# Zero fills of two stages issued in pairs, and w_down moved in 2-KB rows

## The chip, the core and the metric

The kernel runs on one core of one Trainium2 chip. The metric is the device time of one execution in microseconds (us), as the median of several runs. TensorE (PE), VectorE (DVE), ScalarE (ACT) and GpSimd (POOL) compute; SyncE (SP) and POOL issue transfers. Sixteen DMA engines carry out all transfers of the core, whichever engine issued them.

## What is computed

The reference is one decode step of a transformer block and its gradients for all inputs but one:

```
mod = (silu(c) @ w_mod) -> sa, ca, ga, sb, cb, gb          # six vectors of 1024
h = layernorm(x) * (1 + ca) + sa
x = x + ga * (attention(h @ wq, K, V) @ wo)                # last W = 4096 of 65536 cache rows
h = layernorm(x) * (1 + cb) + sb
x = x + gb * ((sigmoid(h @ w_gate) * (h @ w_up)) @ w_down) # F = 3584
out = x, and the vjp with grad_out for x, K, V, wq, wo, w_gate, w_up, w_down, c, w_mod
```

There is one query row, 32 query heads, 4 key/value heads of width 128, and D = 1024. The gradients of the two caches have 4 x 65536 x 128 elements in bf16 each. Only the last 4096 rows of each head are not zero. So 120 MB (in units of 1024 x 1024 bytes) of the outputs are zeros that must still be written, and they are about half of all bytes that move.

## The kernel before

**Zero fills.** The regions that are zero are cut into 120 pieces of 1 MB: 8 head regions of 15 pieces. A piece is `[128 partitions x 4096 bf16]`, 8 KB per partition. The source is one small tile, `zeros`, of 2 KB per partition in an 8-bit type, which the DMA widens to 32 bits as it writes. The list `zleft` holds the pieces in order. Eight of them are "narrow": they are written as two transfers[...] (L160 to L165). The other 112 are "wide", one transfer each (L169). `zero(n, after)` takes n pieces off the list and issues them from POOL. If `after` is given, the first waits for that matmul, so that fills are paced by the progress of TensorE.

**The stages.** All engines execute fixed orders of instructions, written by hand. In the order of time the stages are:

- loads, modulation vectors, transposes of K and wq, scores and softmax (to about 75 us), with 8 fills (`Z_Q`, `Z_SM`);
- **N** (about 75 to 155 us): 128 steps s, each with two matmuls at L635; in every step `zero(Z_N[s], recent(mm, 6))` issues fills that wait for the matmul of five steps before;
- **B** (about 155 to 270 us): 48 chunks of eight matmuls at L687; each ends in `zero(Z_B[chunk], recent(mm, 3))`. Three fills stand in its middle (`Z_GA`);
- **CB and FOLD** (about 270 to 303 us): three fills (`Z_CB`), then `fold_tile` (L882), the loads of the first two feed-forward blocks (`load_ug`, L869) and the fills of `Z_FOLD`;
- **the feed-forward blocks** (about 295 to 480 us): seven blocks q of 512 columns. For each, `front` (L933) and `ffn_mm` (L950) are the forward products, `wd_ttr` and `wd_outer` make the gradient of w_down in place, and a loop over j makes those of w_up and w_gate in place. `store_wd` (L859) and `store_ug` (L873) write them out from POOL. `load_wd` (L856) is issued from SP and waits until the store of the block before has left the buffer. `dug_part` spreads a vector over the partitions, with a copy on ACT at L970. Each block has 4 fills, the last two blocks 6 (`Z_FFN`);
- **the end** (from about 480 us): gradients of wo, w_mod, K, V and wq, with the last fills (`Z_END`, and what is left in the list).

**Queues.** POOL issues 273 transfers into one queue. Each of these transfers counts on one of eight semaphores in turn, and a POOL transfer waits until the one eight before it has landed. SP has a queue of its own.

**w_down.** Row 2p and row 2p + 1 of a half block of 256 rows lie on partition p, so that a partition's piece of 4 KB is contiguous in memory. For the same reason `front` takes every second column of w_up and w_gate, and the copy at L970 permutes its elements.

Of the kernel before, what the change touches and what calls it, by code (L numbers as in the profile page):

```python
# [10 lines left out]
P = 128  # L11
FP32 = mybir.dt.float32
# [10 lines left out]
FB = 512  # L23
# [17 lines left out]
def spread(total, n):  # L41
    return [(i + 1) * total // n - i * total // n for i in range(n)]
# [7 lines left out]
Z_Q = [0] * 6 + [1, 3]  # L50
Z_KC = [0] * 8
Z_SM = 4
Z_N = spread(29, 128)
Z_B = spread(29, 43) + [1, 1, 1, 1, 0]
Z_FOLD = (3, 2, 2)
Z_FFN = [(1, 1, 1, 1)] * 5 + [(1, 1, 2, 2), (2, 2, 1, 1)]
Z_END = (2, 1, 1, 0, 0)
@with_exitstack
def kernel(
# [26 lines left out]
    nc = tc.nc  # L86
# [17 lines left out]
    def vt(shape, name, dt=FP32):  # L104
        return pool.tile(shape, dt, name=name)
# [4 lines left out]
    ZW = 4096  # L110
    zeros = vt([P, ZW // 2], "zeros", FP8)
# [11 lines left out]
    zregions = []  # L123
    for og in (out_2, out_3):
        for g in range(G):
            region = og[0, g, 0:SKW, :].rearrange("r d -> (r d)").rearrange("(p x) -> p x", p=P)
            for i in range(region.shape[1] // ZW):
                zregions.append(region[:, i * ZW:(i + 1) * ZW])

    narrow = zregions[0:len(NARROW)]
# [1 line left out]
    zleft = []  # L133
# [13 lines left out]
    def dep(later, earlier):  # L147
        tc.add_manual_dep(later.ins, earlier.ins.name,
                          mybir.DependencyInfo(mybir.DependencyClass.Sync, mybir.DependencyReason.DATA),
                          reason="pace")  # L150

    def zero(n, after=None):
        for _ in range(n):
            if len(zleft) <= keep[0]:
                return
            region, narrow_ = zleft.pop(0)
            first = None
            if narrow_:
                nc.gpsimd.inc_swdge_sem([], [], mode="reset_dge_cursor")  # L160
                n = nlen - ncount.pop()
                first = nc.gpsimd.dma_start(
                    out=rest[0:NS, 0:nlen * 128].rearrange("p (t x) -> p t x", t=2)[:, :, n * 64:(n + 1) * 64],
                    in_=zeros[0:NS, 0:64].rearrange("p (t x) -> p t x", t=1).broadcast_to([NS, 2, 64]))
                ins = nc.gpsimd.dma_start(  # L165
                    out=region[8:P, :].bitcast(FP32).rearrange("(t p) x -> p t x", t=2),
                    in_=zeros[0:60, :].rearrange("p (t x) -> p t x", t=1).broadcast_to([60, 2, ZW // 2]))
            else:
                ins = nc.gpsimd.dma_start(out=region.bitcast(FP32), in_=zeros[:, :])  # L169
            if after is not None:  # L170
                dep(first or ins, after)

# [15 lines left out]
    def new_tp(name="tp"):  # L188
        p, tag = next_pool()
        return p.tile([P, 1024], BF16, name=name, tag=tag)  # L190
# [214 lines left out]
    for j in range(KD):  # L405
        for k in range(16):
            mm = nc.tensor.matmul(mod_ps[:, k:k + 1], lhsT=wm01_t[j][:, k * P:(k + 1) * P],
                                  rhs=cs_bf[:, j:j + 1], start=(j == 0 and k == 0), stop=(j == KD - 1),
                                  skip_group_check=True)
# [53 lines left out]
    for j in range(KD):  # L463
# [6 lines left out]
        for h in range(HQ):  # L470
            mm = nc.tensor.matmul(q_ps[:, h:h + 1], lhsT=wq_t[j][:, h * P:(h + 1) * P],  # L471
                                  rhs=h1_bf[:, j:j + 1], start=(j == 0 and h == 0), stop=(j == KD - 1),
                                  skip_group_check=True)
# [9 lines left out]
    for ch in range(8):  # L483
        ps = new_ps("sc_ps")
        for g in range(G):
            mm = nc.tensor.matmul(ps[32 * g:32 * g + 32, 0:512], lhsT=q_col2[:, HG * g:HG * g + 32],
                                  rhs=k_T[:, g, ch * 512:(ch + 1) * 512], start=True, stop=True,
                                  tile_position=(0, 32 * g))
# [19 lines left out]
    for tb in range(4):  # L508
# [3 lines left out]
        tp = new_tp("tp_pT")  # L512
# [107 lines left out]
    def recent(mm, lag):  # L620
        last_mm.append(mm)
        return last_mm[-lag] if len(last_mm) >= lag else last_mm[0]

    for g in range(G):
        nbank = bank_pair("n_ps", g)
        for t_ in range(KT):
            s = g * KT + t_
            vp = vp_t[(s // 2) % 2]
            if t_ % 2 == 0:
                tt(vp.rearrange("p t h d -> p (t h d)"),  # L630
                   v_nat[:, g, t_ * DH:(t_ + 2) * DH].rearrange("p (t o d) -> p t o d", t=2, o=1).broadcast_to([P, 2, HG, DH]),
                   pT2[:, g, HG * t_:HG * t_ + 2 * HG, :].rearrange("p n (o k) -> p n o k", o=1).broadcast_to([P, 2 * HG, 64, 2]),
                   ALU.mult)
            for k in range(2):
                mm = nc.tensor.matmul(nbank[k][:, :], lhsT=k_nat[:, g, t_ * DH:(t_ + 1) * DH],  # L635
                                      rhs=vp[:, t_ % 2, 4 * k:4 * k + 4, :].rearrange("p h d -> p (h d)"),
                                      start=(t_ == 0), stop=False)
            zero(Z_N[s], recent(mm, 6))
            if t_ == 20:
                build_bd(g)  # L640
            if s == 2:
                ok_cols(ok4)
            elif s == 4:
                ok_rows()
            elif s == 24:
                mod_gb()
            elif t_ % 2 == 1:
                side()
        for k in range(2):
            nc.tensor.matmul(nbank[k][:, :], lhsT=nkb_rows[:, :], rhs=bd[:, 4 * k:4 * k + 4, :].rearrange("p h d -> p (h d)"),  # L650
                             start=False, stop=True)
            c0 = (HG * g + 4 * k) * P
            nc.scalar.activation(out=N_sb[:, c0:c0 + 512], in_=nbank[k][:, :], func=ACT.Copy, scale=float(SCALE))
        load_wo(4 + g, nc.gpsimd if g == 3 else nc.sync)
        if g < 3:
            jobs.extend(t_unit(h, "AA") for h in range(HG * g, HG * g + HG))
# [5 lines left out]
    bq = []  # L662
# [11 lines left out]
    nbq = len(bq)  # L674
    bbank = {}

    def bch(n=1):
        for _ in range(n):
            if not bq:
                return  # L680
            p, i, u = bq.pop(0)
            if i == 0:
                bbank[p] = bank_pair("b_ps", p)
            for a in range(4):
                h = 4 * u + a
                for k in range(2):
                    mm = nc.tensor.matmul(bbank[p][k][:, :], lhsT=a4[:, p, h, :], rhs=wo_t[u][:, a, k * 512:(k + 1) * 512],  # L687
                                          start=(i == 0 and a == 0), stop=(i == 7 and a == 3))
            zero(Z_B[nbq - 1 - len(bq)], recent(mm, 3))
            if i == 7:  # L690
                for k in range(2):
                    o = B_t[p][:, k * 512:(k + 1) * 512]
                    if k == 0 or p == NBP - 1:
                        nc.scalar.copy(out=o, in_=bbank[p][k][:, :])
                    else:
                        cp(o, bbank[p][k][:, :])
# [152 lines left out]
    ug_v = arena[:, 16 * KIB:48 * KIB].rearrange("p (h q j k f) -> p q h j k f", h=2, q=2, j=4, k=2)  # L849
    wd_v = ar(152, 8).rearrange("p (i d) -> p i d", i=4)  # L850

    def wd_dram(t, q, s):
        return t[q * FB + s * 256:q * FB + s * 256 + 256, :].rearrange("(p j) d -> p j d", j=2)

    def load_wd(q, s):
        nc.sync.dma_start(out=wd_v[:, 2 * s:2 * s + 2, :], in_=wd_dram(B_w_down, q, s))  # L856
# [40 lines left out]
    load_ug(0, 4, 4)  # L897
    zero(Z_FOLD[0])
    side(2)
# [12 lines left out]
    load_ug(1, 4, 4)  # L912
    zero(Z_FOLD[1])
    bcast(dffn_bf, KD, b1k, "AV")

    dug_b = scr
# [10 lines left out]
    def front(q):  # L927
        gu = gu_t[q % 2]
        for col, k in ((4, 0), (0, 1)):
            for i in range(4):  # L930
                f0 = 256 * (i // 2) + i % 2
                for j in range(KD):
                    nc.tensor.matmul(gu[:, col + i:col + i + 1], lhsT=ug_v[:, q % 2, j // 4, j % 4, k, f0:f0 + 255:2],  # L933
                                     rhs=h2_bf[:, j:j + 1], start=(j == 0), stop=(j == KD - 1))

    def gates(q):
# [26 lines left out]
    def dug_part(q):  # L963
        r = small[q % 2]
        mulv(r["dug_bf"][:, 0:4], r["dhh"], r["sg"])
        mulv(r["dug_bf"][:, 4:8], r["dhh"], r["hom"])
        tp = new_tp("tp_dug")
        for i in range(8):
            nc.tensor.transpose(tp[:, i * P:(i + 1) * P], r["dug_bf"][:, i:i + 1].broadcast_to([P, P]), ident_bf[:, :])
        nc.scalar.copy(out=dug_b.rearrange("p (s f j) -> p s f j", s=4, j=2),  # L970
                       in_=tp.rearrange("p (s j f) -> p s f j", s=4, j=2))

    for h in range(HQ):
        jobs.append(tr_unit(wo_t[h // 4][:, h % 4, :]))
# [9 lines left out]
    ffn_mm(0, 1)  # L984
    wd_ttr(0, 1)
    dug_part(0)
    wd_outer(0, 1)
    zero(Z_FOLD[2])
    load_wd(1, 0)
    load_wd(1, 1)  # L990
    for q in range(NB):
# [290 lines left out]
    s2(6)  # L1282
    s2(7)
    keep[0] = 0
    zero(len(zleft))
    assert not zleft and not narrow and not jobs and not bq

# [28 lines left out]
```

## Time and profile before

| | |
|---|---|
| median of three runs | 603.95 us (603.56 to 604.6) |
| the profiled execution | 604.6 us, of which 602.8 us are the span shown |
| bytes moved by DMA | 248.19 MB in 47730 packets |
| HBM read, written | 61.87 MB, 185.60 MB |
| zero fills | 112 of 1024 KB and 8 of 960 KB, median 13.9 and 13.1 us from issue to landing |
| w_down loads | 14 of 512 KB, median 9.7 us from issue to landing |
| busy: PE, DVE, ACT, POOL | 65%, 54%, 47%, 29% |

The page divides the span into 40 slices of 15.07 us. In its row "DMA", 9 means that the 16 DMA engines were busy for at least 90% of the slice; the row "GB/s" is what they moved in it. A landing is the moment at which the last of the 16 DMA engines has reported. In a timeline, the square brackets hold the idle time of the engine just before the instruction, and what ended it.

### The profile page before, as it was taken

The page shows a single profiled execution, that of the slowest core. Times are in us where ns is not written, and L with a number is a line of the kernel's source. Part 1 is how long each engine was busy: PE and PEld are TensorE (multiplying, and loading weights), DVE is VectorE, ACT ScalarE, POOL GpSimd, SP SyncE. Part 2 cuts the span into 40 slices and gives each one's busy share as a digit, 9 for nine tenths or more (in the row PEclk, how much of TensorE's full clock was granted, in tenths as well). Part 3 has the DMA queues.
Part 4 walks back from the last instruction along what each step waited for, and adds up shares of the span by engine and source line. Part 5 has one row for each costly group of instructions (what it writes and reads, how often), then busy time and mean ns, then how long its engine had stood idle before and what let it go on. Part 6 is the DMA issues. An engine that isn't in the chain of part 4 may idle for free.

```text
span 602.8 us, 10936 instructions
## 1 busy us (share of the span) xinstructions
PE 389.8 (65%) x4516; PEld 265.6 (44%) x4516; DVE 324.8 (54%) x616; ACT 282.8 (47%) x426; POOL 174.2 (29%) x281
## 2 busy tenths in 40 slices
PE   3997789999999989989433434352533377837200
PEld 3995434334344445548433433342433255736200
DVE  3654498999511010060374675846768279678510
ACT  2489514567202014218273847657476834744100
POOL 0002121212322212213334454455443431132230
PEclk9999699999999989989755555555555586655555
DMA  8999999999999999999999999999999999999996
GB/s 351 421 417 421 406 426 413 413 417 422 421 422 427 423 426 419 407 426 417 406 413 411 412 415 413 413 409 410 414 416 421 422 419 411 423 424 426 424 415 256
DMA packets 47730, 248.19 MB, mean 412 GB/s; under 512 B 5629, under 2 KB 5629, under 8 KB 27264
## 3 DMA queue, kind: packets, MB, share of 16 engines
q0 software_dynamic: 37792, 210.78, 91.0%
q1 hardware_dynamic: 9840, 36.71, 18.0%
q8 instruction: 35, 0.57, 0.4%
q14 instruction: 15, 0.12, 0.1%
q10 hardware_dynamic: 48, 0.01, 0.0%
HBM read 61.87 MB, written 185.60 MB: 411 GB/s over the span
## 4 chain that ended last, share of the span: by engine, by line
DMA 35%; PE 34%; DVE 14%; issue 7%; ACT 5%; POOL 2%; ACTq 0%; POOLq 0%; DVEq 0%; SPq 0%
DMA out_dram<-arena 17%; PE b_ps L687 14%; DMA out_dram<-zeros 8%; DMA arena<-in_B_w_down_dram 7%; PE n_ps L635 6%; DVE arena L210 4%; DVE arena L193 4%; PE t_ps L597 2%; DMA arena<-in_B_w_up_dram 2%; DVE arena L206 2%; DVE junk L210 2%; ACT arena L241 2%; PE tp_wq L453 2%; PE w_ps L394 1%; PE tp_k L434 1%
## 5 line engine op out<-in xcount | busy, mean ns | idle before, releaser
L169 POOL DMA_DIRECT2D out_dram<-zeros x112 | 61.1, 546 | 205.6 <-PE q_ps L471 50.2
L687 PE MATMUL b_ps<-arena 128*128 128x512 bf16 x384 | 89.5, 389 | 0.0
L836 PE MATMUL tp_side<-ident_bf,arena 128*128 128x128 bf16 x416 | 50.1, 297 | 53.7 <-ACT arena L837 44.6
L193 DVE TENSOR_TENSOR arena<-arena 128x2048 bf16<-128x2048 bf16 x64 | 76.6, 1224 | 2.2 <-PE n_ps L635 0.3
L837 ACT COPY arena<-tp_side 128x1024 bf16<-128x1024 bf16 x52 | 52.0, 1010 | 46.0 <-PE tp_side L836 45.8
L210 DVE CUSTOM_DVE_ANT_0 arena<-arena,scr 128x1024 bf16<-128x1024 bf16 x56 | 65.2, 1221 | 9.5 <-ACT scr L970 9.5
L635 PE MATMUL n_ps<-arena 128*128 128x512 bf16 x256 | 65.7, 378 | 6.5 <-DVE arena L193 4.8
L836 PEld LDWEIGHTS <-arena 128*128 128x128 bf16 x416 | 41.2, 137 | 59.2 <-issue 59.1
L241 ACT ACTIVATE arena<-scr,h 128x1024 bf16<-128x1024 bf16 x56 | 61.0, 1146 | 0.0
L687 PEld LDWEIGHTS <-arena 128*128 128x128 bf16 x384 | 37.7, 100 | 46.4 <-issue 7.1
L873 POOL DMA_DIRECT2D out_dram<-arena x42 | 30.7, 733 | 43.9 <-ACT arena L241 36.7
L635 PEld LDWEIGHTS <-arena 128*128 128x128 bf16 x256 | 24.6, 97 | 41.8 <-issue 16.4
L210 DVE CUSTOM_DVE_ANT_0 junk<-arena,b1k 128x1024 bf16<-128x1024 bf16 x28 | 34.3, 1223 | 15.9 <-DMA arena<-in_B_w_down_dram 15.4
L1137 ACT ACTIVATE arena<-ps_kv 128x512 bf16<-128x512 f32 x48 | 26.2, 694 | 29.8 <-PE ps_kv L1133 26.0
L599 ACT CAST arena<-t_ps 128x512 bf16<-128x512 f32 x56 | 30.1, 589 | 12.1 <-PE t_ps L597 12.1
L1133 PE MATMUL ps_kv<-junk,arena 8*128 8x128 bf16 x256 | 27.5, 306 | 10.1 <-DVE arena L206 9.4
L1133 PEld LDWEIGHTS <-arena 8*128 8x128 bf16 x256 | 25.5, 141 | 11.9 <-issue 11.9
L202 DVE CAST arena<-b_ps 128x512 bf16<-128x512 f32 x5 | 3.5, 692 | 47.1 <-PE b_ps L687 47.1
L933 PE MATMUL fg<-h_bf,arena 128*128 128x1 bf16 x448 | 15.6, 166 | 19.0 <-DMA arena<-in_B_w_up_dram 12.4
L455 ACT COPY arena<-tp_wq 128x1024 bf16<-128x1024 bf16 x23 | 21.7, 1044 | 8.0 <-PE tp_wq L453 8.0
L950 PE MATMUL fg<-hh_bf,arena 128*128 128x1 bf16 x224 | 8.0, 166 | 24.1 <-DMA arena<-in_B_w_down_dram 23.4
L933 PEld LDWEIGHTS <-arena 128*128 128x128 bf16 x448 | 14.4, 105 | 20.2 <-DMA arena<-in_B_w_up_dram 13.0
(297 smaller groups left out, 640.0 us busy)
## 6 DMA issues: line engine op xcount, KB each, us to landing
out_dram<-zeros POOLq DMA_DIRECT2D x112, 1024.0 KB, 13.9
out_dram<-arena POOLq DMA_DIRECT2D x32, 1024.0 KB, 18.8
out_dram<-arena POOLq DMA_DIRECT2D x36, 512.0 KB, 10.3
arena<-in_A_wq_dram SPq DMA_DIRECT2D x8, 1024.0 KB, 20.0
out_dram<-zeros POOLq DMA_DIRECT2D x8, 960.0 KB, 13.1
arena<-in_B_w_down_dram SPq DMA_DIRECT2D x14, 512.0 KB, 9.7
out_dram<-arena POOLq DMA_DIRECT2D x28, 256.0 KB, 10.9
arena<-in_A_wo_dram SPq DMA_DIRECT2D x6, 1024.0 KB, 24.8
```

The lines of the kernel that those rows point to most:

```text
L169: ins = nc.gpsimd.dma_start(out=region.bitcast(FP32), in_=zeros[:, :])
L193: return nc.vector.tensor_tensor(out=out, in0=a, in1=b, op=op)
L210: return nc.vector.tensor_tensor_reduce(out=out, in0=w, in1=b, scale=1.0, scalar=0.0, op0=ALU.mult, op1=ALU.add, accum_out=acc)
L241: return nc.scalar.activation(out=out, in_=b, func=ACT.Copy, scale=col)
L599: nc.scalar.copy(out=o, in_=ps)
L635: mm = nc.tensor.matmul(nbank[k][:, :], lhsT=k_nat[:, g, t_ * DH:(t_ + 1) * DH], rhs=vp[:, t_ % 2, 4 * k:4 * k + 4, :].rearrange("p h d -> ...
L687: mm = nc.tensor.matmul(bbank[p][k][:, :], lhsT=a4[:, p, h, :], rhs=wo_t[u][:, a, k * 512:(k + 1) * 512], start=(i == 0 and a == 0), stop= ...
L836: nc.tensor.transpose(tp[:, i * P:(i + 1) * P], blk[:, i * P:(i + 1) * P], ident_bf[:, :])
L837: nc.scalar.copy(out=blk, in_=tp[:, :])
L873: nc.gpsimd.dma_start(out=ug_part(view, q, j0, n), in_=ug_tile(q, k, j0, n))
L933: nc.tensor.matmul(gu[:, col + i:col + i + 1], lhsT=ug_v[:, q % 2, j // 4, j % 4, k, f0:f0 + 255:2], rhs=h2_bf[:, j:j + 1], start=(j == 0) ...
L1133: nc.tensor.matmul(ps[:, t4 * DH:(t4 + 1) * DH], lhsT=rows[32 * g:32 * g + HG, t_ * P:(t_ + 1) * P], rhs=hd[32 * g:32 * g + HG, :], start= ...
```

## The change

Two sets of edits stand in the diff.

Fills in the stages N and B, and the last ones, may be issued as pairs: `zero` has a new argument `most`, and where the next piece on the list is the wide neighbour of the same region, one transfer writes both (`wide_fill`). Such a transfer reads `zeros` twice and writes 16 KB per partition, 2 MB in all. `Z_N` and `Z_B` are calls now, and a call issues one or two pieces: N has 17 calls (29 before), B has 18 (33 before). Narrow pieces and the ends of regions break some pairs. Counted through the list, N issues 28 pieces (29 before), B 31 (33 before), CB, the blocks and the end as many as before, and 4 pieces in two transfers are left for the very end (1 before). Of the 112 wide pieces 52 go out as 26 pairs and 60 alone.

w_down moves in single rows: row p and row 128 + p of a half block lie on partition p, in pieces of 2 KB. `front` takes consecutive columns, and the copy at L970 is a plain one. The two fills that stood behind the first block's w_down stores (the third entry of `Z_FOLD`) stand ahead of them, in the second entry.

```diff
-Z_N = spread(29, 128)
-Z_B = spread(29, 43) + [1, 1, 1, 1, 0]
-Z_FOLD = (3, 2, 2)
+Z_N = spread(17, 128)
+Z_B = spread(16, 43) + [1, 0, 1, 0, 0]
+Z_FOLD = (3, 4)
...
+    def wide_fill(region, i, n):
+        return nc.gpsimd.dma_start(
+            out=region[:, i * ZW:(i + n) * ZW].bitcast(FP32).rearrange("p (t x) -> p t x", t=n),
+            in_=zeros[:, :].rearrange("p (t x) -> p t x", t=1).broadcast_to([P, n, ZW // 2]))
+
-    def zero(n, after=None):
+    def zero(n, after=None, most=1):
...
             else:
-                ins = nc.gpsimd.dma_start(out=region.bitcast(FP32), in_=zeros[:, :])
+                m = 1
+                while m < most and zleft and not zleft[0][1] and zleft[0][0][0] is region and zleft[0][0][1] == i + m:
+                    zleft.pop(0)
+                    m += 1
+                ins = wide_fill(region, i, m)
...
-            zero(Z_N[s], recent(mm, 6))
+            zero(Z_N[s], recent(mm, 6), 2)
...
-            zero(Z_B[nbq - 1 - len(bq)], recent(mm, 3))
+            zero(Z_B[nbq - 1 - len(bq)], recent(mm, 3), 2)
...
     def wd_dram(t, q, s):
-        return t[q * FB + s * 256:q * FB + s * 256 + 256, :].rearrange("(p j) d -> p j d", j=2)
+        return t[q * FB + s * 256:q * FB + s * 256 + 256, :].rearrange("(j p) d -> p j d", p=P)
...
             for i in range(4):
-                f0 = 256 * (i // 2) + i % 2
                 for j in range(KD):
-                    nc.tensor.matmul(gu[:, col + i:col + i + 1], lhsT=ug_v[:, q % 2, j // 4, j % 4, k, f0:f0 + 255:2],
+                    nc.tensor.matmul(gu[:, col + i:col + i + 1], lhsT=ug_v[:, q % 2, j // 4, j % 4, k, i * P:(i + 1) * P],
...
-        nc.scalar.copy(out=dug_b.rearrange("p (s f j) -> p s f j", s=4, j=2),
-                       in_=tp.rearrange("p (s j f) -> p s f j", s=4, j=2))
+        nc.scalar.copy(out=dug_b, in_=tp[:, :])
...
     wd_outer(0, 1)
-    zero(Z_FOLD[2])
     load_wd(1, 0)
...
     keep[0] = 0
-    zero(len(zleft))
+    zero(len(zleft), None, 2)
```

More of the change, by code (lines that the diff above doesn't have):

```diff
@@ L127 @@
             for i in range(region.shape[1] // ZW):
-                zregions.append(region[:, i * ZW:(i + 1) * ZW])
+                zregions.append((region, i))
     narrow = zregions[0:len(NARROW)]
@@ L156, in zero @@
                 return
-            region, narrow_ = zleft.pop(0)
+            (region, i), narrow_ = zleft.pop(0)
             first = None
@@ L165, in zero @@
                 ins = nc.gpsimd.dma_start(
-                    out=region[8:P, :].bitcast(FP32).rearrange("(t p) x -> p t x", t=2),
+                    out=region[8:P, i * ZW:(i + 1) * ZW].bitcast(FP32).rearrange("(t p) x -> p t x", t=2),
                     in_=zeros[0:60, :].rearrange("p (t x) -> p t x", t=1).broadcast_to([60, 2, ZW // 2]))
             else:
-                ins = nc.gpsimd.dma_start(out=region.bitcast(FP32), in_=zeros[:, :])
+                m = 1
[3 more added lines that the diff above has]
+                ins = wide_fill(region, i, m)
             if after is not None:
```

## The prediction

> **What bounds the kernel now.** I read the page first: the DMA row, then packets, then the chain of waits.
>
> ```profile
> span 602.8 us, 10936 instructions
> ...
> DMA  8999999999999999999999999999999999999996
> GB/s 351 421 417 421 406 426 413 413 417 422 421 422 427 423 426 419 407 426 417 406 413 411 412 415 413 413 409 410 414 416 421 422 419 411 423 424 426 424 415 256
> DMA packets 47730, 248.19 MB, mean 412 GB/s; under 512 B 5629, under 2 KB 5629, under 8 KB 27264
> ...
> DMA 35%; PE 34%; DVE 14%; issue 7%; ACT 5%; POOL 2%; ACTq 0%; POOLq 0%; DVEq 0%; SPq 0%
> ```
>
> No compute engine is busy over 65% of the span, but the 16 DMA engines are busy from the first slice to the last. 248 MB at 412 GB/s is the span itself. So a transfer that moves earlier or later costs nothing so long as the engines always have something issued. Time is lost in two ways only: bytes that take longer, and moments in which nothing issued is left. I call what is issued and not yet moved **the stock**.
>
> Windows show where the rate is below its best (columns: us; busy PE, PEld, DVE, ACT, POOL; clock; DMA share; GB/s):
>
> ```profile
> 76.00:94.00 18.00, 14.05 (x116) 6.27 (x117) 15.51 (x28) 2.88 (x10) 3.40 (x7) 1.00 1.15 426
> 96.00:120.00 24.00, 22.84 (x101) 9.83 (x101) 23.21 (x21) 14.32 (x31) 5.58 (x10) 1.00 1.16 412
> 160.00:250.00 90.00, 86.86 (x634) 44.62 (x633) 12.28 (x37) 19.09 (x27) 20.73 (x36) 0.98 1.13 423
> 300.00:480.00 180.00, 71.44 (x1006) 61.52 (x1007) 113.48 (x241) 115.60 (x126) 80.80 (x122) 0.50 1.12 414
> ```
>
> Fills alone run at 426, the B stage at 423, the feed-forward blocks at 414. The waits of the SP queue and a piece of the chain tell why the blocks are lower:
>
> ```profile
> SPq L856 <- DMA out_dram<-arena: 156.1, 12, 41.4
> ```
> ```profile
> 392.05 9.82 DMA arena<-in_B_w_down_dram
> ...
> 401.89 1.23 DVE junk L210
> ...
> 407.86 10.78 DMA out_dram<-arena
> ...
> 418.70 9.67 DMA arena<-in_B_w_down_dram
> ```
>
> Each w_down load waits for the store that frees its buffer; the store lands 10.8 us after issue, the load 9.7 us after that, and compute takes what is left. It is a loop without slack: the first j-loop products of blocks 1 to 6 (332.41 to 458.56 us in the timeline) are 25.2 us apart. A block moves 10 MiB, 10.49 MB, so 416 GB/s; at 423 it would take 24.8 us.
>
> **What the Trainium skill says.** "DMA: Bandwidth & Descriptors", section "Queues, rings and completion order": each DMA engine takes turns between its queue rows, a packet at a time. The trace agrees: a 512-KB w_down load needs 9.7 us beside the POOL queue. Same page, "Where 436 GB/s comes from": 435 GB/s is the ceiling of the 16 engines; 426 over fills is near it, so little is left to win. Same page, "Specifications": about 1 us to the first byte of a POOL-issued DMA. Here the first fill ends its issue at 49.8 us and its queue's first packet record starts at 51.9, so I use 2.1 us.
>
> **The change, part by part.**
>
> *Issues.* 112 wide fills become 26 pairs and 60 singles: 26 transfers fewer, 11 pairs in N, 13 in B, 2 at the end. A wide fill's data packets stay 8 KB. Only completions go: one 4-byte packet per engine and transfer, 9 to 52 ns in the packet records. 26 x 9 to 52 ns is 0.2 to 1.4 us of each engine; they overlap data, so I take -0.5. POOL issues (0.55 us each) were hidden under waits for PE (44.6 us on n_ps alone) and stay so.
>
> *Stock in N and B.* N issues 28 fills for 29, B 31 for 33, so 3.1 MB less is issued by the end of B. FOLD keeps 7, but four stand before the first block's w_down stores instead of two; those stores and the block's queue are then behind 2 MB more and 3.1 less, about the same. Three fills go to the very end: a last 4 MB instead of 1, at 2.45 us each 7.35 us of work moved, not added. The question is whether the stock lasts.
>
> At the start of N:
>
> ```profile
> 75.46 0.67 POOL L165 DMA_DIRECT2D out_dram<-zeros  x1
> 76.96 0.58 POOL L169 DMA_DIRECT2D out_dram<-zeros  x1 [0.83 <-PE n_ps L635]
> 81.42 0.56 POOL L169 DMA_DIRECT2D out_dram<-zeros  x1 [3.87 <-PE n_ps L635]
> 83.76 0.53 POOL L169 DMA_DIRECT2D out_dram<-zeros  x1 [1.78 <-PE n_ps L635]
> ```
>
> The narrow fill at 75.46 lands 10.2 us later, 85.7. Afterwards it is issued at step 7 (about the same moment) and the next, a pair, at step 15, between these steps 13 (81.42) and 17 (83.76), at 82.6; with 0.6 of issue and 2.1 its first byte comes at 85.3. That just meets 85.7: no loss, or up to 1 us on engines that are ahead.
>
> At the end of B:
>
> ```profile
> 265.07 0.53 POOL L169 DMA_DIRECT2D out_dram<-zeros  x1 [1.40 <-PE b_ps L687]
> 270.25 0.77 POOL L338 DMA_DIRECT2D arena<-in_w_mod_dram  x1 [4.65 <-PE b_ps L687]
> 271.01 0.53 POOL L169 DMA_DIRECT2D out_dram<-zeros  x1
> ```
>
> The fill at 265.07 lands after 13.3 us, at 278.3. Three fills fewer make that 271.0. The next transfer waits for PE until 270.25, so its first byte is at 273.1: **2.1 us with nothing to move**. Then the section load, three CB fills and a w_down load (4.7 MB, 11.2 us) last to 284.3, past the first block's loads (280.10 + 2.8). I take +2.1; 0 if the landing is that of the slowest engine only, 5 if a constant 420 GB/s holds and the stock also fails at 84 and 265 us.
>
> *w_down in 2-KB pieces.* Loads: 14 x 128 packets of 4 KB become 14 x 256 of 2 KB. Packet records: 159 ns for 4 KB from the SP queue, 84 for 2 KB (the wo loads), so 9 ns more for each 4 KB: 1792 x 9 / 16 = **+1.0 us**. Stores: POOL packs rows into 4-KB packets, and the dwo stores, also 2-KB rows, show 159 ns: 0, at most another 1.0. POOL's issue of a store has 0.56 us and takes at most the 0.73 of L873.
>
> The turns cost more than the bytes. A load has 8 packets per engine now and 16 then; eight more turns of the other queue, about 5.4 KB or 205 ns each at that mix, make it land 1.6 us later. On a loop without slack that is up to 9.9 us in six blocks. But the skipped turns go to the POOL queue, whose store in the same loop then lands as much earlier, as long as there is stock. What cannot be given back is the thinner stock: I take 0.2 us for each of seven blocks, half of the 0.4 us by which a block already misses 423 GB/s, **+1.4**, between 0 and 9.9.
>
> *Layouts.* L933's weights lose their step of two; L950, without step, also loads in 105 ns. The dug copy at L970 loses its permutation: 1012 ns against 1010 for the plain copy L837. 0 each, and they lie beside DMA.
>
> *Sum.* -0.5 + 2.1 + 1.0 + 1.4 = +4.0 on the profiled execution: span 602.8, 604.6 with the 1.8 around it, so 608.6. The median of the runs, 603.95, is 0.65 lower: **608.0 us**.
>
> **Rivals.**
> - *Worse (0.20):* the feed-forward loop doesn't use the thinner stock to run ahead; then 7.35 - 2.1 = 5.2 us of the moved fills are exposed at the end, or w_down's delay stays half on the path (5 us): 613 to 618. For: no slack in that loop. Against: DVE is busy only 63% there (113.48 of 180 us), so it can follow faster landings.
> - *No difference (0.10):* slow engines always keep stock; -0.5 + 1.0: about 604.5.
> - *Faster (0.15):* fewer completions and longer runs of writes raise the rate of N's mixed stretch from 412 towards 426. 80 us of N at +2% is -1.6, the completions at most -1.4; with +1.0 for w_down 602. It decides if no pair is issued after the stock is gone. Against: 26 transfers fewer leave all data packets as they were.
> - *The pairs are not made:* narrow fills and region ends break some, as counted above; the remaining 26 are in the program. Nothing is left to it.
>
> **How the numbers follow.** The likeliest case, 0.55, spans 605.5 to 612. With the worse case's lower part and the faster case's upper part the range is 602.8 to 613.5. What a measurement can tell from no change is about 0.2%, 1.2 us. Faster 0.15, same 0.10, slower 0.75.
>
> **What would show it.** Right: about 49,100 packets; 26 zero transfers of 2 MB; a dip in GB/s near 271 us; w_down loads landing after 11 us or more; the last slices longer by fills. Wrong: GB/s without dip and blocks at 25.2 us or less (then only bytes count), or a slice above 430 in N or B (then pairs do pay).

## The result: slower by 8.3 us

| | before | after |
|---|---|---|
| median of six runs | 604.05 us (603.54 to 604.98) | 612.58 us (610.16 to 614.35) |
| the profiled execution | 604.6 us, span 602.8 | 610.53 us, span 608.8 |
| ratio after / before | | 1.0137, 95% interval 1.0108 to 1.0167 |

The ratio amounts to +8.3 us (6.5 to 10.1), twice the +4.0 forecast; the forecast's sign was right, its size was not. The profiled execution is one of the fastest of the six: it is 5.9 us longer than that of before, and what is read from the trace below accounts for these 5.9. From the page of the kernel after (span; DMA busy tenths and GB/s in 40 slices of 15.22 us; packets; shares of the chain):

```profile
span 608.8 us, 10875 instructions
...
DMA  9999999999999999999999999999999999999997
GB/s 354 419 416 421 405 426 411 412 421 420 421 428 426 423 410 386 404 360 395 395 418 406 385 404 413 406 412 411 410 415 420 424 416 415 424 423 426 420 415 291
DMA packets 49105, 248.18 MB, mean 408 GB/s; under 512 B 5213, under 2 KB 5213, under 8 KB 28640
...
PE 35%; DMA 30%; DVE 17%; ACT 7%; issue 6%; POOL 1%; ACTq 0%; POOLq 0%; DVEq 0%; SPq 0%
```

The row of tenths shows no gap, the row of GB/s does: 386 in the slice from 228 us, 360 from 259 us, 385 from 335 us. The bytes are the same, so this is time in which less was moved. The prediction's windows, now in the kernel after (last columns: clock, DMA share, GB/s):

```profile
76.00:94.00 18.00, 14.28 (x115) 6.48 (x116) 15.61 (x21) 2.88 (x10) 2.19 (x3) 1.00 1.15 423
96.00:120.00 24.00, 22.95 (x103) 9.84 (x102) 23.13 (x20) 15.50 (x33) 3.98 (x6) 1.00 1.17 414
160.00:250.00 90.00, 86.85 (x640) 44.96 (x638) 11.64 (x35) 18.88 (x26) 15.54 (x23) 0.98 1.12 415
300.00:480.00 180.00, 70.73 (x1007) 60.88 (x1008) 111.60 (x235) 115.50 (x127) 82.95 (x121) 0.50 1.09 409
```

In this execution the start of N is unhurt (423 for 426, 414 for 412). B fell from 423 to 415, the feed-forward blocks from 414 to 409. The waits of the SP queue and the same piece of the chain:

```profile
SPq L865 <- DMA out_dram<-arena: 158.4, 12, 44.5
```
```profile
390.71 11.44 DMA arena<-in_B_w_down_dram
...
402.18 1.23 DVE junk L219
...
406.17 10.46 DMA out_dram<-arena
...
416.69 10.95 DMA arena<-in_B_w_down_dram
```

The loads in this piece take 11.44 and 10.95 us for 9.82 and 9.67, the store 10.46 for 10.78, so the loop lives on, with a slower load. To place the loss, here are four thin places, the first four lines of the kernel before and the next four of the kernel after:

```profile
227.00:235.00 8.00, 8.00 (x78) 4.89 (x77) 1.38 (x2) 3.20 (x4) 2.65 (x4) 1.00 1.14 421
249.00:253.00 4.00, 3.72 (x38) 2.24 (x36) 0.96 (x3) 0.46 (x1) 2.29 (x4) 1.00 1.10 398
269.00:275.00 6.00, 4.23 (x56) 3.23 (x55) 1.00 (x2) 4.53 (x6) 2.35 (x4) 1.00 1.13 415
283.00:289.00 6.00, 5.90 (x101) 5.42 (x99) 0.57 (x4) 4.91 (x8) 1.83 (x4) 1.00 1.10 410
```
```profile
227.00:235.00 8.00, 8.00 (x83) 5.08 (x81) 0.69 (x1) 3.52 (x4) 2.45 (x4) 1.00 0.99 325
249.00:253.00 4.00, 4.00 (x21) 1.81 (x19) 0.00 (x0) 0.00 (x0) 1.59 (x4) 1.00 1.02 345
269.00:275.00 6.00, 4.64 (x72) 4.16 (x72) 0.00 (x0) 4.97 (x7) 2.17 (x4) 1.00 0.88 265
283.00:289.00 6.00, 5.99 (x118) 5.63 (x117) 0.58 (x4) 4.53 (x7) 1.85 (x4) 1.00 1.06 376
```

Difference in GB/s times length gives what was not moved: 0.77, 0.21, 0.90 and 0.20 MB. At 423 GB/s that is 1.8, 0.5, 2.1 and 0.5 us, together 4.9, and 2.1 MB is all that the first 305 us lose (windows further below). The second and the fourth place are as thin in e4 (341 and 384 GB/s), a kernel that takes no longer than before. So only the places at 227 and 271 us, 1.7 MB or 3.9 us, are shown to be the change's work. What happened in the thin place at 271 us, from POOL's timeline of the kernel after:

```profile
261.90 0.72 POOL L154 DMA_DIRECT2D out_dram<-zeros  x1 [8.31 <-PE b_ps L696]
268.80 0.77 POOL L347 DMA_DIRECT2D arena<-in_w_mod_dram  x1 [6.18 <-PE b_ps L696]
269.56 1.61 POOL L154 DMA_DIRECT2D out_dram<-zeros  x3
```

After the pair at 261.90 POOL issued nothing until B's last matmul released the section load at 268.80. At 227 us the pattern is the same: a pair at 216.75 us, the next transfer at 226.48.

### The profile page after: what moved, and what is told of

It reads as the page before. It is cut to its first block, busy times and chain, and to the rows that moved or that the text cites. A ratio compares the mean times of both kernels' runs of the same rounds, so it can differ in the third digit from the quotient of the medians.

```text
span 608.8 us, 10875 instructions
## 1 busy us (share of the span) xinstructions
PE 386.7 (64%) x4516; PEld 265.0 (44%) x4516; DVE 325.8 (54%) x616; ACT 282.5 (46%) x426; POOL 169.4 (28%) x255
## 2 busy tenths in 40 slices
DMA packets 49105, 248.18 MB, mean 408 GB/s; under 512 B 5213, under 2 KB 5213, under 8 KB 28640
## 4 chain that ended last, share of the span: by engine, by line
PE 35%; DMA 30%; DVE 17%; ACT 7%; issue 6%; POOL 1%; ACTq 0%; POOLq 0%; DVEq 0%; SPq 0%
DMA out_dram<-arena 15%; PE b_ps L696 14%; DMA arena<-in_B_w_down_dram 9%; PE n_ps L644 6%; DVE arena L215 4%; DVE arena L202 4%; DVE arena L219 3%; DVE junk L219 3%; DMA out_dram<-zeros 2%; PE t_ps L606 2%; ACT arena L250 2%; DMA arena<-in_B_w_gate_dram 2%; PE w_ps L403 2%; PE tp_wq L462 2%; PE tp_k L443 1%
## 5 line engine op out<-in xcount | busy, mean ns | idle before, releaser
L154 POOL DMA_DIRECT2D out_dram<-zeros x86 | 52.0, 606 | 191.3 <-PE q_ps L480 50.9
L845 PEld LDWEIGHTS <-arena 128*128 128x128 bf16 x416 | 41.1, 137 | 56.3 <-issue 56.0
L696 PEld LDWEIGHTS <-arena 128*128 128x128 bf16 x384 | 37.7, 100 | 46.2 <-issue 6.8
L644 PEld LDWEIGHTS <-arena 128*128 128x128 bf16 x256 | 24.6, 97 | 41.8 <-issue 16.4
L608 ACT CAST arena<-t_ps 128x512 bf16<-128x512 f32 x56 | 30.1, 589 | 12.1 <-PE t_ps L606 12.1
L958 PEld LDWEIGHTS <-arena 128*128 128x128 bf16 x224 | 7.1, 104 | 41.3 <-DMA arena<-in_B_w_down_dram 39.2
L662 ACT ACTIVATE arena<-n_ps 128x512 bf16<-128x512 f32 x8 | 4.3, 594 | 34.5 <-PE n_ps L659 34.5
## 6 DMA issues: line engine op xcount, KB each, us to landing
arena<-in_B_w_down_dram SPq DMA_DIRECT2D x14, 512.0 KB, 10.5
```

The lines of the kernel that those rows point to most:

```text
L154: return nc.gpsimd.dma_start(out=region[:, i * ZW:(i + n) * ZW].bitcast(FP32).rearrange("p (t x) -> p t x", t=n), in_=zeros[:, :].rearrang ...
L608: nc.scalar.copy(out=o, in_=ps)
L845: nc.tensor.transpose(tp[:, i * P:(i + 1) * P], blk[:, i * P:(i + 1) * P], ident_bf[:, :])
```

## The experiments

Two theories stood at first. **Count**: with three fills fewer by the end of B the queue runs dry, and the work that was not done then is added at the end. **Pairing**: a transfer of 2 MB, or the moment at which it is issued, costs time. Later runs took the slack, the w_down rows and the order in FOLD apart. Microseconds below are the ratio minus 1 times the median of before in the same comparison.

| run | median (runs) | before | ratio, 95% interval | us |
|---|---|---|---|---|
| e1_pairs_only | 610.38 (5) | 603.91 | 1.0100 (1.0082 to 1.0119) | +6.0 |
| e2_fewer_singles | 609.49 (6) | 603.91 | 1.0098 (1.0075 to 1.0121) | +5.9 |
| e3_wd_rows | 605.68 (8) | 603.91 | 1.0030 (1.0020 to 1.0039) | +1.8 |
| e4_pairs_lead | 603.84 (13) | 603.91 | 0.9995 (0.9988 to 1.0003) | -0.3 |
| e5_fewer_one | 604.93 (20) | 604.23 | 1.0014 (1.0006 to 1.0021) | +0.85 |
| e6_ga_back | 606.84 (4) | 604.23 | 1.0046 (1.0028 to 1.0063) | +2.8 |
| e7_ffn_light | 605.90 (7) | 604.23 | 1.0031 (1.0019 to 1.0043) | +1.9 |
| e8_cb_back | 608.73 (4) | 604.23 | 1.0079 (1.0055 to 1.0102) | +4.8 |
| e9_fewer_late | 611.30 (4) | 604.26 | 1.0111 (1.0088 to 1.0134) | +6.7 |
| e10_fold_ahead | 604.86 (20) | 604.26 | 1.0011 (1.0004 to 1.0018) | +0.66 |
| e11_wd_load_rows | 605.20 (13) | 604.26 | 1.0016 (1.0008 to 1.0025) | +1.0 |
| e12_wd_store_rows | 604.55 (20) | 604.26 | 1.0008 (1.0002 to 1.0015) | +0.5 |

### e1: the pairs and counts alone

The kernel after, with w_down and the order in FOLD as before:

```diff
-Z_N = spread(29, 128)
-Z_B = spread(29, 43) + [1, 1, 1, 1, 0]
+Z_N = spread(17, 128)
+Z_B = spread(16, 43) + [1, 0, 1, 0, 0]
 Z_FOLD = (3, 2, 2)
...
+                ins = wide_fill(region, i, m)
```

> The fills of the changed kernel (17 calls in N, 18 in B, pairs, 4 MB left for the end), but w_down in 4-KB pieces and the two fills of Z_FOLD behind the first block's w_down stores, as before. Theory 1 (the stock runs out in B and at the end of B, and the three fills that were not issued there are exposed at the end): 608.5 to 611 us, with dips of GB/s near 228 and 270 us. Rival (w_down's 2-KB rows cost most of the 8.5 us): 604 to 606. Rival (the two fills of Z_FOLD in front of the first block's stores cost 3 us or more): 606 to 609.

Measured: +6.0 us, most of the +8.3. Two windows of e1:

```profile
227.00:235.00 8.00, 8.00 (x69) 4.72 (x68) 1.38 (x2) 2.98 (x4) 2.97 (x4) 1.00 0.89 296
269.00:275.00 6.00, 4.54 (x50) 3.10 (x48) 2.04 (x4) 3.50 (x5) 2.36 (x4) 1.00 0.82 260
```

The same two holes as in the kernel after, 1.0 and 0.9 MB against before.

### e2: as many fewer, but all single

```diff
-Z_N = spread(29, 128)
-Z_B = spread(29, 43) + [1, 1, 1, 1, 0]
+Z_N = spread(28, 128)
+Z_B = spread(29, 43) + [1, 0, 1, 0, 0]
```

> The kernel before with 28 fills in N, 31 in B and 4 left for the end, all still issued one by one: the stock is thinner by three fills, but no fill waits for its partner. Theory 1 in its strong form (the count alone does it): 607 to 610. If it is the waiting for a partner that empties the stock: 604 to 606.5, with no dip near 228 us and a small one near 270. If only the 2-MB transfer itself matters: 604.

Measured: +5.9 us, with no pair in the program, against +6.0 in e1. The count is the cause; that the pairs add something can't be told from these two medians. In e2 the holes lie later, so here are wider windows (the profiled execution was its slowest, 613.25 us):

```profile
219.00:241.00 22.00, 19.85 (x151) 10.91 (x150) 3.56 (x17) 6.97 (x10) 4.77 (x8) 0.92 1.09 394
241.00:263.00 22.00, 20.19 (x226) 12.22 (x225) 1.60 (x7) 6.47 (x8) 4.75 (x8) 1.00 1.06 366
263.00:281.00 18.00, 16.14 (x134) 9.58 (x133) 9.72 (x16) 7.12 (x11) 2.87 (x5) 0.91 0.88 307
```

The same windows move 421, 413 and 419 GB/s in before and 365, 409 and 359 in e1. Against before, e2 misses 0.6, 1.0 and 2.0 MB, and e1 1.2, 0.1 and 1.1. The pairs decide where the stock runs out first: what isn't lost at the first place is lost at the next ones, and the medians of the two kernels agree.

### e3: the w_down rows alone

```diff
-        return t[q * FB + s * 256:q * FB + s * 256 + 256, :].rearrange("(p j) d -> p j d", j=2)
+        return t[q * FB + s * 256:q * FB + s * 256 + 256, :].rearrange("(j p) d -> p j d", p=P)
```

with `front` and the dug copy as in the kernel after.

> The kernel before with w_down moved in single rows of 2 KB (loads, stores, the columns that the forward products take, the plain copy), fills as before. The prediction's terms: +1.0 us of bytes and +1.4 of thinner stock, 605.5 to 607. If turns at the DMA engines stay on the path of the loop: 609 or more, block pitch over 26 us. If the loop gives it all back: 604 to 605.

Measured: +1.8 us (1.2 to 2.4).

### e4: pairs that lead

As many fills as before, and each pair is issued where the first of its two pieces was due, so that the stock is never thinner than before:

```diff
+            if ahead[0]:
+                ahead[0] -= 1
+                continue
...
+                ahead[0] = m - 1
+                ins = wide_fill(region, i, m)
```

> The kernel before with pairs that are issued when the first of the two fills was due, so that at no moment fewer fills are out than before; counts per stage as before, w_down and Z_FOLD as before. Theory 1: no dip, 603 to 604.7 us. If a 2-MB transfer itself costs time (it keeps loads behind it waiting): 606 or more. If half the completions are worth what the prediction's faster case says: 602.5 or less.

Measured: 0.9995, no difference from before that can be told (-0.7 to +0.2 us). The program has the same 26 transfers of 2048 KB as the kernel after. A window that was 265 in the kernel after:

```profile
269.00:275.00 6.00, 4.23 (x51) 3.03 (x49) 3.06 (x6) 4.16 (x6) 1.84 (x3) 1.00 1.15 429
```

While the queue is kept full, pairs neither help nor harm by more than these 0.7 us.

### e5 and e9: how much slack there is at the end of B

One fill fewer in B's last chunks, and three fewer there, all single, nothing else changed:

```diff
-Z_B = spread(29, 43) + [1, 1, 1, 1, 0]
+Z_B = spread(29, 43) + [1, 0, 1, 1, 0]      # e5
+Z_B = spread(29, 43) + [1, 0, 0, 0, 0]      # e9
```

> The kernel before with one fill fewer in B (its place is the second of the five calls at the end of B), all single, two fills left for the end instead of one. Theory (the thinnest place of the kernel before is at 250 us, 1.60 MB of stock, used up at 253.8 by 16 engines together while the next transfer's first byte comes at 252.2, so 1.6 us of slack; each fill taken away is 2.45 us): 2.45 - 1.6 = +0.9, so 604.8 us. That fill goes after 250, so if the place at 271 counts (5.2 us of slack): 603.9. If every fill left for the end is simply exposed: 606.4.

> The kernel before with three fills fewer, all three taken from the last 15 us of B (256, 263 and 265 us), four left for the end. Only the place at 271 us, the one that the prediction worked out, can run dry. The prediction's way to measure slack there (landing of the last fill at 278.3, next first byte at 273.1, 5.2 us) gives 7.35 - 5.2 = 2.1, so 606.2 us. If slack is what 16 engines together have left (1.84 MB at 271.0, used up at 275.4, 2.3 us or less): a loss of 5 to 6 us, 609 to 610.

Measured: e5 +0.85 us for a fill of 2.45 us, e9 +6.7 us for three of 7.35 us together, more than the 609 to 610 us expected. So the slack at 271 us is about 1.6 us by e5 (1.2 to 2.1) and 0.65 by e9 (2.0 at most), and not 5.2. That e5 met its expected 604.8 is luck in part: that figure was the slack at 250 us, but the fill that e5 leaves out falls due at 256 us, and in its execution 0.5 MB are missing from 263 to 281 us (390 GB/s for 419). How e9 (its slowest execution, 613.28 us) loses the time, POOL's timeline first, then the windows:

```profile
257.23 0.53 POOL L169 DMA_DIRECT2D out_dram<-zeros  x1 [1.19 <-PE b_ps L687]
273.17 0.77 POOL L338 DMA_DIRECT2D arena<-in_w_mod_dram  x1 [15.41 <-PE b_ps L687]
```
```profile
267.00:269.00 2.00, 2.00 (x11) 0.88 (x9) 2.00 (x4) 0.00 (x0) 0.00 (x0) 1.00 0.99 360
269.00:271.00 2.00, 2.00 (x11) 0.89 (x10) 2.00 (x4) 0.00 (x0) 0.00 (x0) 1.00 0.07 20
271.00:273.00 2.00, 1.88 (x9) 0.77 (x8) 1.94 (x4) 0.30 (x1) 0.00 (x0) 1.00 0.00 0
273.00:275.00 2.00, 1.18 (x22) 1.18 (x22) 0.00 (x0) 1.31 (x3) 1.83 (x4) 1.00 0.42 33
275.00:277.00 2.00, 1.49 (x22) 1.17 (x20) 0.00 (x0) 2.00 (x3) 0.52 (x1) 1.00 0.71 223
```

The last fill landed 14.0 us after issue, at 271.24, where the prediction put it (271.0). But the rate was 360 from 267 and 20 from 269 us: up to the landing 1.0 MB less was moved than at 423 GB/s, 2.4 us' worth. The trace keeps the reports of the 16 DMA engines one by one, and they say why. For this fill 15 engines reported between 268.85 and 269.77 us and one alone at 271.24.

The restart came to what was assumed. The section load was issued at 273.17; 0.77 of issue and 2.1 more give 276.0, and 0.51 MB had been moved by 277, 1.2 us' worth. Its first packets start earlier, at 274.65, but take up to 1.3 us each.

In this execution B also ended 2.9 us later than in that of before. Another 0.6 MB are missing from 241 to 263 us (386 GB/s for 413), before the first missing fill was due; e4 (391) and e12 (401), which have all fills there, show a part of that dip too.

### e6 and e8: give the fills back

e6 is the kernel after with `Z_GA` 6 for 3, three fills more in the middle of B. e8 is e2 with `Z_CB` 6 for 3, three fills more just behind the hole.

```diff
-Z_GA = 3
+Z_GA = 6      # e6
-Z_CB = 3
+Z_CB = 6      # e8
```

> The changed kernel with three more fills in the middle of B (Z_GA 6 instead of 3, near 178 us), so that the three fills that it lacks are out again before the thin places. Theory (count and time of fills alone make the loss, not the pairs): what stays is w_down's rows and the order in FOLD, 605.3 to 607 us. If pairs cost time of themselves or empty the stock at 227 us by coming late: 608 or more.

> The kernel of the second experiment (28 and 31 single fills) with the three missing fills given back behind B (Z_CB 6 instead of 3, near 271 us), so that the end has one fill again. If the loss is made by engines standing still before 271 us, it is made by then and stays: 607.5 to 609.5. If the loss is only that fills stand exposed at the end: 604 to 605.

Measured: e6 +2.8 us, so three fills ahead of the hole take 5.5 of the 8.3 us away. What is left is about what the w_down rows and the order in FOLD cost by themselves (1.8 + 0.66 = 2.5). e8 +4.8 us, against +5.9 for e2, and the intervals overlap: three fills behind the hole win back little or nothing. The hole at 271 us stays in e8:

```profile
269.00:275.00 6.00, 4.14 (x62) 3.51 (x61) 0.21 (x1) 5.30 (x7) 3.92 (x7) 1.00 0.66 188
```

### e7: do the blocks run ahead?

The rival *worse* said that the feed-forward loop keeps its pitch when fewer fills share the queue, so that moved fills are exposed. e7 takes one fill from each of five blocks and moves them to the end, 12.25 us of work:

```diff
-Z_FFN = [(1, 1, 1, 1)] * 5 + [(1, 1, 2, 2), (2, 2, 1, 1)]
+Z_FFN = [(1, 1, 1, 0)] * 5 + [(1, 1, 2, 2), (2, 2, 1, 1)]
```

> The kernel before with three fills instead of four in each of the first five feed-forward blocks; five more are left for the very end. The prediction held that the blocks run ahead when there is less to move before them: then the block pitch falls from 25.2 towards 22.8 us and the total stays at 604 to 606. If the blocks keep their pace whatever the stock: pitch 25 us and 5 x 2.45 = +12 us, 614 to 616.

Measured: +1.9 us, not +12. Forward products of block 1 and of block 5, in the timeline of before and then of e7:

```profile
344.14 1.68 PE L933 MATMUL fg<-h_bf,arena 128*128 128x1 bf16 x57 [0.91 <-DMA arena<-in_B_w_gate_dram]
...
446.43 1.68 PE L933 MATMUL fg<-h_bf,arena 128*128 128x1 bf16 x57 [0.92 <-DMA arena<-in_B_w_gate_dram]
```
```profile
344.29 1.68 PE L933 MATMUL fg<-h_bf,arena 128*128 128x1 bf16 x57 [0.80 <-DMA arena<-in_B_w_gate_dram]
...
438.13 1.68 PE L933 MATMUL fg<-h_bf,arena 128*128 128x1 bf16 x57 [0.81 <-DMA arena<-in_B_w_gate_dram]
```

Four blocks take 102.3 us in before and 93.8 in e7, 2.1 us less for each; a fill is worth 2.45. The blocks do run ahead, at 408 GB/s for 414 (305 to 466 us). The rival's mechanism is not the cause.

### e10: the two fills of FOLD ahead of the stores

```diff
-Z_FOLD = (3, 2, 2)
+Z_FOLD = (3, 4)
...
     wd_outer(0, 1)
-    zero(Z_FOLD[2])
```

> The kernel before with the two last fills of Z_FOLD ahead of the first block's w_down stores. The prediction: 0, because fewer fills stand before them; alone it puts 2 MB, 4.9 us, before these stores. If the blocks make that good later: 604 to 605 us, with a longer first block (31 us or more between the first two j-loops) and a shorter second. If not: 607 to 609.

Measured: +0.66 us (0.2 to 1.1). The landing of the first block's two w_down stores, in before, after and e10 in this order (from each one's view of the storing line, 299 to 309 us):

```profile
DMA to landing us min/median/max: 10.4/10.7/11.0
```
```profile
DMA to landing us min/median/max: 14.6/14.7/14.8
```
```profile
DMA to landing us min/median/max: 13.0/13.0/13.1
```

The stores free the buffers for the next two loads, which thus begin later. From the first j-loop to the second it takes 27.0 us in before, 30.6 in e10 and 32.0 in the kernel after; the next interval gives most of it back (25.2, 22.1 and 22.2 us). The order isn't the only thing that stretches the first interval: it is 30.1 us in e3 too, whose stores land in 10.8 us.

### e11 and e12: loads or stores of w_down alone

Only `load_wd`, or only `store_wd`, moves in 2-KB rows.

```diff
     def load_wd(q, s):      # e11
-        nc.sync.dma_start(out=wd_v[:, 2 * s:2 * s + 2, :], in_=wd_dram(B_w_down, q, s))
+        nc.sync.dma_start(out=wd_v[:, 2 * s:2 * s + 2, :], in_=B_w_down[q * FB + s * 256:q * FB + s * 256 + 256, :].rearrange("(j p) d -> p j d", p=P))
...
     def store_wd(q, s):      # e12
-        nc.gpsimd.dma_start(out=wd_dram(out_8, q, s), in_=wd_v[:, 2 * s:2 * s + 2, :])
+        nc.gpsimd.dma_start(out=out_8[q * FB + s * 256:q * FB + s * 256 + 256, :].rearrange("(j p) d -> p j d", p=P), in_=wd_v[:, 2 * s:2 * s + 2, :])
```

> The kernel before with only the loads of w_down in single 2-KB rows; stores stay in 4-KB pieces, so the rows of w_down are in another order within a half block, in what the forward products take and in the gradient. The prediction: bytes +1.0 and turns +1.4 lie in the loads, 605.5 to 606.5 us, nearly all of the 1.8 that rows cost together. If the stores are what costs: 604 to 604.7.

> The kernel before with only the stores of w_down's gradient in single 2-KB rows; loads stay in 4-KB pieces, so the gradient's rows are in another order within a half block. The prediction: 0 at the DMA engines (packets stay 4 KB), POOL's issue 0.56 to 0.73 us: 604 to 604.6 us. If rows of 2 KB cost in the stores too: 605 or more.

Measured: loads +1.0 us (0.5 to 1.5), less than expected, stores +0.5 (0.1 to 0.9), together 1.5 of e3's 1.8. Median landing of a w_down load: 9.7 us in before, 10.7 in e11 and in e3, 10.0 in e12.

### The sum

e1 + e3 + e10 is 6.0 + 1.8 + 0.66 = 8.5 us, against 8.3 measured.

## Why the prediction was right and wrong, point by point

- **What bounds the kernel**: right. No compute wait had to change for the time to change; e2 alters only when transfers are issued, and costs 5.9 us.
- **The place of the hole, at 271 us**: right. **The step that failed is the size of the fills' term, +2.1 us; it measured 6.0 (e1) and 5.9 (e2).** The prediction counted 7.35 us of moved fills less 5.2 us of slack, the distance from the last landing (278.3) to the next first byte (273.1). e9 takes three fills away right there and loses 6.7 of the 7.35.

  A landing is the report of the slowest engine. In the kernel before, the 16 reports for the fill of 265.07 came between 274.37 and 278.32 us, on average at 275.84. In e9, where nothing stood behind the last fill, each engine's completion packet starts 0.4 to 0.5 us before its report. So the engines were through with the fill of 265.07 at 275.4 us on average, and their mean slack was 2.3 us, not 5.2; that of single engines lay between 0.8 and 4.8. An estimate from these 16 reports: one fill fewer costs 0.6 us, on the engines with less than 2.45 us of slack (e5: 0.85, 0.4 to 1.3), and three cost 5.1 (e9: 6.7, 5.3 to 8.1). What e9 loses beyond that is not placed; the later end of B in its execution is one candidate.

  The kernel after bears this out. The pair at 261.90 landed at 272.0, and the next first byte was due at 268.80 + 0.77 + 2.1 = 271.7: no hole at all by the prediction's rule. But the 16 reports came at 270.0 on average, which leaves an engine 2.1 us without work, and the window from 269 us misses 0.9 MB, 2.1 us' worth. "0 if the landing is that of the slowest engine only" had the sign of this correction backwards: the earlier the other engines end, the larger the hole.

  The Trainium skill, "DMA: Bandwidth & Descriptors", section "Anatomy of one DMA — SWDGE (gpsimd) path", puts most of a transfer's fixed 2 us on the confirmation of the last write before the semaphore fires. Here it is less: in e9 the slowest engine's last 8-KB packet starts at 270.40 us, and its report comes 0.8 us later. The mean of the 16 reports lies 1.9 us before the last one, so most of the 2.4 us in e9 is the spread between the engines.
- **The second half of that error: one place stood for all.** The prediction worked out 84 and 271 us. The window at 227 us, where B's fills stand far apart, loses 1.8 us in the kernel after. The prediction's upper bound, 5 us for a stock that also fails elsewhere, was nearly the measured value.
- **N's start**: no loss in the profiled execution of the kernel after. But e1 and e6, with the same fills in N, move 411 and 402 GB/s from 76 to 94 us for 426, 0.6 and 1.0 us' worth. N's first pair came at 83.64 and 84.08 us there and at 81.19 in the kernel after. "No loss, or up to 1 us" holds as a range.
- **-0.5 for 26 fewer completions**: neither seen nor excluded. e4 has the 26 pairs and measures -0.7 to +0.2 us.
- **w_down, +1.0 and +1.4**: 2.4 forecast, 1.8 measured, which is near for partly wrong reasons. The loads cost +1.0 in all (e11), the value that the packet records gave. Their landings came 1.0 us later, and nothing of the +1.4 on top is seen. The stores, taken at 0, cost 0.5. e12 has 47,731 packets, one more than before, so its stores do stay in packets of 4 KB; what their 0.5 us is stays open.
- **FOLD's order, taken at 0**: 0.66. By "Behind 2 MB more and 3.1 less, about the same" the stores should have landed no later. They landed 4.0 us later in the kernel after and 2.3 us later in e10: the fills that were missing took nothing off the queue in front of the stores. That their time had been lost at the holes before fits, but no run tests it alone.
- **Rivals.** *Worse* (613 to 618) had the number nearly right for a wrong reason: e7 shows that the blocks run ahead. Most of the loss lies earlier, before 305 us. Windows of before, of after and of e1, in this order (clock, DMA share, GB/s last):

```profile
0.00:305.00 305.00, 262.03 (x2645) 156.96 (x2646) 144.50 (x236) 125.27 (x225) 64.28 (x116) 0.95 1.12 415
```
```profile
0.00:305.00 305.00, 261.65 (x2659) 157.93 (x2659) 147.10 (x242) 127.47 (x227) 55.12 (x90) 0.96 1.11 408
305.00:466.00 161.00, 64.23 (x957) 55.17 (x956) 104.95 (x213) 101.14 (x112) 73.66 (x107) 0.50 1.09 409
```
```profile
0.00:305.00 305.00, 263.62 (x2645) 158.46 (x2646) 144.50 (x236) 125.47 (x225) 53.48 (x88) 0.96 1.10 405
305.00:466.00 161.00, 66.62 (x968) 57.25 (x968) 107.30 (x220) 103.99 (x115) 73.15 (x111) 0.50 1.14 414
```

  Seven GB/s less over 305 us is 2.1 MB, 5 us; e1's ten are 3.1 MB. From 305 to 466 us e1 is at 414, as before is; only the kernel after, with w_down's rows and FOLD's order, falls to 409, another 0.8 MB or 1.9 us. About 1 us of the whole comes back at the very end, where the last slice moves 291 GB/s and that of before 256. 5.0 + 1.9 - 1.0 is the 5.9 us between the two profiled executions. *Faster* fell with e4. No run was faster than before; e4 equals it.
- **The account.** The sum of e1, e3 and e10 lies 4.5 us above the forecast. 3.9 of it are the fills' term, 0.5 the completions, 0.7 FOLD's order, and w_down gives 0.6 back.
- **Signs.** Seen: 49,105 packets, 26 transfers of 2 MB, the dip at 271 us, 291 GB/s in the last slice. Loads after 11 us or more: half seen, 10.5 in the median.

## What to carry to other kernels

Where a kernel is bound by its transfers, count what is issued and not yet moved, in bytes, at every point at which the issuing engine waits; don't read the slack from a landing, which is the report of the slowest engine, when the others may have been idle for microseconds. In this kernel the size of a transfer, 1 or 2 MB, made no difference while the queue was full, but its moment did: a pair must be issued when its first half was due. Three fills given back ahead of the dry moment took the loss away (e6), three just after it left most of it (e8).

## What was unexpected of the hardware

**A dry queue brings the clock's variation to light.** The kernel before keeps within 1.5 us in its six runs (603.5 to 605.0) and within 1.8 in the 48 of the last comparison; the kernel after spreads over 4.2 us (610.16 to 614.35), e2 over 4.6. B's last matmul ends at different times in different executions. It goes with the granted clock from 45 to 120 us, the third column from the right, here in the profiled executions of the kernel after and of e2:

```profile
45.00:120.00 75.00, 61.12 (x568) 32.41 (x566) 56.56 (x80) 41.25 (x88) 13.87 (x22) 0.95 1.14 415
```
```profile
45.00:120.00 75.00, 62.47 (x539) 32.09 (x536) 52.23 (x75) 37.23 (x80) 15.43 (x27) 0.86 1.13 417
```

With 0.95 the section load, which waits for B's last matmul, went out at 268.8 us (after), 269.4 (e3), 269.45 (e8) and 271.35 (e7, whose clock from 240 to 268 us was 0.88 for 0.94), with 0.93 between 270.25 and 271.28 (before, e10, e11, e5, e1), with 0.89 at 272.24 (e12), 273.17 (e9) and 270.62 (e4, 1.00 for 0.94 from 240 to 268 us), with 0.86 at 272.9 (e6) and 273.34 (e2). While transfers are waiting, this is hidden: e12's B ended 2.0 us later than that of before, and its execution took 605.25 us for 604.6, hardly more than its median difference of 0.5. With a dry queue it shows: e2's execution took 613.25 us, 3.8 above its median. This is a relation over single executions; no run set the clock.

**The 16 engines don't end a transfer together.** In the kernel before, with a full queue, their reports for one fill lie 4.0 us apart (274.37 to 278.32), and one engine reports 1.5 us behind the other 15 (276.86 and 278.32); so it does in e9 (269.77 and 271.24). Why one is slower stays open.

**Rows of 2 KB become packets of 2 KB from SP and of 4 KB from POOL.** e11 has 1792 packets more than before, e12 one. The same 7.3 MB in 2-KB rows cost 1.0 us as loads from SP and 0.5 us as stores from POOL; the intervals (0.5 to 1.5, 0.1 to 0.9) overlap, so that the loads cost more isn't shown.

**26 transfers of 2 MB in place of 52 of 1 MB changed nothing measurable** while others waited behind them (0.9995, e4).
